# A fused attention and MoE kernel: other rules for interleaving its MoE pieces, a new order of the first blocks, and the last output tile in two halves

## The chip, the cores and the metric

The kernel runs on one core of a Trainium2 chip. The metric is the device time of one execution in microseconds, taken as the median over runs; the kernel before takes 360.17 us (median of 8 runs, 359.39 to 360.54). Engine names are those of the profile: PE multiplies matrices, PEld loads its weights, DVE and ACT are the vector and the scalar engine, POOL is GpSimd, and SP issues DMAs. Each engine runs its instructions in program order and waits on semaphores where the program needs it.

## What is computed

A forgetting attention (8 batches, 8 heads, 576 positions, head size 64) whose output, with the heads put side by side, is the input of a two-layer SiLU block with 2048 hidden channels:

```python
scores = scale * q @ k.T                      # per batch and head
cum    = cumsum(log(clip(f, 1e-4, 1)))
scores = where(causal, scores + cum[:, None] - cum[None, :], -1e9)
attn   = softmax(scores)
x      = (attn @ v).transpose(0, 2, 1, 3).reshape(4608, 512)
h      = x @ moe_w_in                         # 512 -> 2048
out    = (h * sigmoid(h)) @ moe_w_out         # 2048 -> 512
```

## The kernel before, in words

All of it is written as one stream per engine; the order in which the Python code emits instructions is the order in which each engine runs them (`tc.manual_schedule`, line 54). There is no planner that looks at times. What interleaves the two halves of the work is a small accounting function, `fill`, described below.

**Attention.** The decay is folded into the values: each value row and a column of ones beside it is multiplied by a weight computed from `f`, so that one matmul gives numerator and denominator. The 576 positions of a batch are a first block of 128 and a rest of 448.

- *First blocks* (`turn0`, `ban0`, `scores0`, `mask0`, `out0`, `back0`, lines 260 to 365). For each batch b, `turn0(b)` transposes the q and k heads with 32 small matmuls into two PSUM tiles `tp` (one copied out by ACT, one by DVE); `scores0` makes the scores of all 8 heads in one tile `sc` and their exp on ACT; `out0` multiplies by the values into `dn0` and divides on DVE; `back0` transposes the result and copies it into an `x` tile for the MoE. For batches 0 to 3 the causal mask is added in PSUM beforehand (`ban0`), for 4 to 7 it is a DVE multiplication (`mask0`). Batches 0 to 3 run back to back at the start (lines 622 to 668), with a few dummy matmuls (`keep_warm`) between them. Batches 4 to 7 run in `one_more` (line 694) with MoE pieces in between: `fill(0.9)` after `turn0`, `fill(2.0)` after the scores, `fill(1.0)` after `out0`.
- *The rest* (the loop at line 756). It runs over 16 pairs m of head pairs, n = 2m and n + 1. Each `scores(n, c)` for c = 0, 1, 2 fills one of two `sc` buffers (pool `psc`, PSUM banks 0 to 3) with 64-row matmuls (line 433) and gives exps to ACT (lines 437, 449) and mask multiplications to DVE (442, 456). Two such chunks stand together, a "burst" here; a cycle m has three bursts, each followed by a `slot`, then `attend(n)` and `attend(n+1)` (tile `dn`, lines 478 and 487) and a fourth `slot`. `back(m-1)` (tile `tx`, line 508) follows the first slot and writes x. `prepare` issues loads and transposes by DMA (SP), casts (POOL) and value products (POOL) for later n.

**MoE.** The 4608 tokens are cut into 13 groups g of 512, 256, 256, 384 x 4, 256, 384 x 4 and 256 tokens. A piece is one of two kinds:

- M1, `m1_chunk(g, fc)`: 4 matmuls into `hp` (line 532, 128 hidden channels of a group), a tanh on ACT (540) and one DVE instruction (541) that writes `gt`. 16 pieces per group.
- M2, `m2_part(g, tb, part)`: 4 matmuls of 512 columns (558), a quarter of one 128-token output tile `po`. The fourth quarter copies the tile to `osb` on ACT (567) and issues its DMA from SP (570), two DMAs of 64 rows where the tile holds the last 64 tokens of two batches. 4 pieces per 128 tokens.

`hp`, `po`, `dn`, `tx` and `tp` share one pool of four PSUM banks (`pbig`, tag "big", banks 4 to 7). A `po` holds its bank from its first quarter until `osb` has read it.

**The accounting.** `fill(us)` adds to a balance and calls `step()` until the balance is used up; each piece is charged 4 x (columns / 2.4 + 2.5) ns. `step()` emits the next M1 of the running order if its group is ready (`ready`, filled when a group's x has been written), or else the next M2 (of an earlier group than the next M1's; M2 is open from `open2` on, after batch 5). Where both are possible, M1 is taken if its share of the group is not ahead of M2's share (lines 597 to 600). `slot` is `fill` with 1.5 us for m < 2 and 2.5 us later, plus the release of groups. After the loop `step()` runs until nothing is left. The last tile is the second 128 tokens of group 12.

Of the kernel before, what the change touches and what calls it, by code (L numbers as in the profile page):

```python
# [10 lines left out]
FP32 = mybir.dt.float32  # L11
BF16 = mybir.dt.bfloat16
P = 128
# [5 lines left out]
def kernel(  # L19
# [10 lines left out]
    nc = tc.nc  # L30

    B, H, S, D = q.shape
    DM, DFF = moe_w_in.shape
    BH = B * H
    NCC = DM // P
    NFC = DFF // P
# [27 lines left out]
    opool = ctx.enter_context(tc.tile_pool(name="opool", bufs=3))  # L64
# [4 lines left out]
    pbig = ctx.enter_context(tc.tile_pool(name="pbig", bufs=4, space=bass.MemoryType.PSUM))  # L69

    w_in_bf = const.tile([P, NCC, DFF], BF16, name="w_in_bf")
    w_out_bf = const.tile([P, NFC, DM], BF16, name="w_out_bf")
# [17 lines left out]
    GW = [4 * P, 2 * P, 2 * P] + [RB] * NM + [NM * ST] + [RB] * (B - NM) + [(B - NM) * ST]  # L90
    NG = len(GW)
# [13 lines left out]
    def rows_of(g, tb):  # L105

        if g < 3:
            b = tb if g == 0 else 4 + 2 * (g - 1) + tb
            return [(slice(0, P), b, 0)]
        for b in range(B):  # L110
            if REST_OF[b] == g:
                return [(slice(0, P), b, P + tb * P)]
        b0 = (0 if g == 3 + NM else NM) + 2 * tb
        return [(slice(0, ST), b0, SM), (slice(ST, P), b0 + 1, SM)]
# [65 lines left out]
    def load_w_in(i):  # L180
        c0, c1 = i * DFF // WQ, (i + 1) * DFF // WQ
        nc.gpsimd.dma_start(out=w_in_bf[:, :, c0:c1], in_=w_in_v[:, :, c0:c1])
# [27 lines left out]
    for i in range(2):  # L210
        for g in range(2):
            nc.vector.tensor_copy(
                out=sel[:, i, :].rearrange("p (u w r) -> p u w r", u=2, w=2)[:, g, :, :],
                in_=ident_bf[:, :].rearrange("p (r u i w) -> p u i w r", u=2, i=2, w=2)[
                    :, g, i, :, :
                ],
            )

    def keep_warm(n):
        t = pbig.tile([P, SM], FP32, name="wm", tag="big")  # L220
        for _ in range(n):
            nc.tensor.matmul(t[:, :], lhsT=warm[:, 0:P], rhs=warm[:, :], start=True, stop=True)
# [4 lines left out]
        out=f_sb[:, :], in0=f_sb[:, :], scalar1=1e-4, scalar2=1.0, op0=ALU.max, op1=ALU.min  # L227
# [32 lines left out]
    def turn0(b, between=0):  # L260
        src = qk0.pop(b)
        qT0[b] = qktp.tile([P, NP, P], BF16, name="qkT", tag="qkT")
        for i, (dst, evac) in enumerate(
            ((qT0[b], nc.scalar.copy), (kT0[b], nc.vector.tensor_copy))
        ):
            if i == 1 and between:
                keep_warm(between)
            tp = pbig.tile([P, NP, NRUN, RUN], FP32, name="tp", tag="big")
            for c in range(RUN):
                for j in range(2):  # L270
                    nc.tensor.matmul(  # L271
                        tp[j * D : (j + 1) * D, :, :, c].rearrange("p a r -> p (a r)"),
                        lhsT=src[:, i, c * D : (c + 1) * D],
                        rhs=sel[:, j, :],
                        start=True,
                        stop=True,
                    )
            evac(
                out=dst[:, :, :].rearrange("p a t -> p (a t)"),
                in_=tp[:, :, :, :].rearrange("p a r c -> p (a r c)"),  # L280
            )

    def ban0(b):
        sc = psc.tile([P, 2, NP, P], FP32, name="sc", tag="sc")
        for i in range(2):
            nc.tensor.matmul(
                sc[:, i, :, :].rearrange("p a t -> p (a t)"),
                lhsT=ident_bf[:, :],
                rhs=ban[:, :, :].rearrange("p a t -> p (a t)"),
                start=True,  # L290
                stop=False,
            )
        return sc
# [31 lines left out]
    def convert_v0(b):  # L325
        nc.gpsimd.tensor_tensor(
            out=v0[b][:, :, :],
            in0=vf0.pop(b)[:, :, :],
            in1=w_bf[:, 0, b * H : (b + 1) * H, None].to_broadcast([P, H, D + 1]),
            op=ALU.mult,  # L330
        )
# [193 lines left out]
    def m1_chunk(g, fc):  # L525
        w = GW[g]
        if fc == 0:
            gts[g] = gpool.tile([P, NFC, w], BF16, name="gt", tag="gt")
        gt = gts[g]
        hp = pbig.tile([P, w], FP32, name="hp", tag="big")  # L530
        for cc in range(NCC):
            nc.tensor.matmul(  # L532
                hp[:, :],
                lhsT=w_in_bf[:, cc, fc * P : (fc + 1) * P],
                rhs=xg(g)[:, cc, :],
                start=(cc == 0),
                stop=(cc == NCC - 1),
            )
        th = tpool.tile([P, w], BF16, name="th", tag="th")
        nc.scalar.activation(out=th[:, :], in_=hp[:, :], func=ACT.Tanh, scale=0.5)  # L540
        nc.vector.scalar_tensor_tensor(  # L541
            out=gt[:, fc, :],
            in0=th[:, :],
            scalar=1.0,
            in1=hp[:, :],
            op0=ALU.add,
            op1=ALU.mult,
        )
# [2 lines left out]

    def m2_part(g, tb, part):
        gt = gts[g]
        if part == 0:
            pos[g, tb] = pbig.tile([P, DM], FP32, name="po", tag="big")
        po = pos[g, tb]
        for fc in range(4 * part, 4 * part + 4):
            nc.tensor.matmul(  # L558
                po[:, :],
                lhsT=gt[:, fc, tb * P : (tb + 1) * P],  # L560
                rhs=w_out_bf[:, fc, :],
                start=(fc == 0),
                stop=(fc == NFC - 1),
            )
        if part == 3:
            osb = opool.tile([P, DM], FP32, name="osb", tag="osb")
            nc.scalar.activation(out=osb[:, :], in_=po[:, :], func=ACT.Copy, scale=0.5)  # L567
            for r, b, s0 in rows_of(g, tb):
                t0 = b * S + s0
                nc.sync.dma_start(out=out[t0 : t0 + r.stop - r.start, :], in_=osb[r, :])  # L570


    M1 = [(g, fc) for g in range(NG) for fc in range(NFC)]
# [5 lines left out]
        else:  # L579
            M2 += [(g, tb, part) for tb in range(nt) for part in range(4)]  # L580
    M2_OF = [sum(1 for x in M2 if x[0] == g) for g in range(NG)]
    at = {"m1": 0, "m2": 0, "left": 0.0}
    ready: set[int] = set()
    open2 = {"w": False}

    def step():

        a, c = at["m1"], at["m2"]
        can1 = a < len(M1) and M1[a][0] in ready
        g1 = M1[a][0] if a < len(M1) else NG  # L590
        g2 = M2[c][0] if c < len(M2) else NG
        if can1 and M1[a][1] == 0 and g1 > g2 + 1:
            can1 = False
        can2 = open2["w"] and c < len(M2) and g2 < g1
        if not can1 and not can2:
            return None
        if can1 and can2:
            f1 = M1[a][1] / NFC
            f2 = (c - sum(M2_OF[:g2])) / M2_OF[g2]
            can1 = f1 <= f2 or g1 > g2 + 1  # L600
        if can1:
            m1_chunk(*M1[a])
            at["m1"] += 1
            return 4 * (GW[g1] / 2.4 + 2.5)
        m2_part(*M2[c])
        at["m2"] += 1
        return 4 * (DM / 2.4 + 2.5)

    def fill(us_):
        at["left"] += us_ * 1000  # L610
        while at["left"] > 0:
            t = step()
            if t is None:
                at["left"] = 0.0
                return False
            at["left"] -= t
        return True
# [7 lines left out]
        out=ban[:, :, :],  # L625
# [6 lines left out]
    weights()  # L632
    setup_pool.__exit__(None, None, None)
    gpool = ctx.enter_context(tc.tile_pool(name="gpool", bufs=2))
    sc = ban0(0)
    scores0(0, sc)
    keep_warm(1)
    convert_v0(0)
    load_w_in(0)
    turn0(1, between=1)  # L640
    sc = ban0(1)
    scores0(1, sc)
    convert_v0(1)
# [49 lines left out]

    def one_more(b):
        turn0(b)
        fill(0.9)
        scores0(b)
        mask0(b)
        fill(2.0)
        out0(b)  # L700
        fill(1.0)
        back0(b, on_act)

    fill(4.0)
# [41 lines left out]

    pending: list = []

    def slot(us_):
        fill(us_)  # L750
        for x in pending:
            x[0] -= 1
        while pending and pending[0][0] == 0:
            ready.update(pending.pop(0)[1])

    for m in range(NQ):
        n = 2 * m
        piece = 1.5 if m < 2 else 2.5
        scores(n, 0)
        scores(n, 1)  # L760
        prepare(n)
        slot(piece)
        if m > 0:
            back(m - 1)
            if m % 2 == 0:
                b = m // 2 - 1
                pending.append([1, [REST_OF[b]] + ([TAILS_OF[b][0]] if b == NM - 1 else [])])
        scores(n, 2)
        scores(n + 1, 0)
        prepare(n + 1)  # L770
        slot(piece)
        scores(n + 1, 1)
        scores(n + 1, 2)
        slot(piece)
        attend(n)
        attend(n + 1)
        slot(piece)
    back(NQ - 1)
    ready.update([REST_OF[B - 1], TAILS_OF[B - 1][0]])
    for x in pending:  # L780
# [34 lines left out]
```

## Time and profile before

| | us |
|---|---|
| Median of 8 runs (lowest to highest) | 360.17 (359.39 to 360.54) |
| The profiled execution | 359.39 |
| Its span, first to last instruction | 357.6 |
| PE busy in the span | 342.8 (96%) |
| ACT, DVE, POOL busy | 217.0, 189.1, 105.0 |
| First M1 starts at | 20.72 |
| First burst of the loop at | 66.52 |
| Last matmul ends at about | 352.6 |

A profile line of a group reads: line, engine, operation, tile written <- tiles read, shape, xcount | busy us, mean ns of one | idle time of the engine just before, and what ended most of it. In a timeline the first two numbers are the start and the length in us (of all xcount instructions together), and a bracket gives the idle time before and what released the instruction. The 40 digits of a slice row are tenths of busy time, or of granted clock for PEclk. The engines overlap consecutive instructions, so lengths of neighbours may add to more than the time they took together.

### The profile page before, as it was taken

What the parts mean: (1) busy time and instruction counts of PE and PEld (TensorE: products, weight loads), DVE (VectorE), ACT (ScalarE), POOL (GpSimd) and SP (SyncE); (2) the same over time, 40 slices, a digit from 0 to 9 for tenths busy, and PEclk for the clock granted to TensorE, in tenths of its full rate; (3) what the DMA queues carried; (4) which work ended last, traced back from release to release, by engine and by line L of the source; (5) the groups of instructions that cost most, each with busy time, mean ns of one, the idle gap of its engine ahead of it and who ended that gap; (6) DMA issues with size and microseconds to landing.
All of it is one profiled execution on the core that took longest, in us unless ns stands there. A gap on an engine that the chain in (4) does not pass through costs nothing.

```text
span 357.6 us, 8999 instructions
## 1 busy us (share of the span) xinstructions
PE 342.8 (96%) x3632; PEld 202.7 (57%) x3632; DVE 189.1 (53%) x409; ACT 217.0 (61%) x398; POOL 105.0 (29%) x183
## 2 busy tenths in 40 slices
PE   7999898899899999999999999999999999999994
PEld 3644465476566556565655675656656655555651
DVE  4467635366466476555656555456755554344320
ACT  5657454667856767668557677595785644454431
POOL 6992145317254136144116207115400000000000
PEclk9999999999999999999999999999999999999999
DMA  9999989599995698698598878289730101001012
GB/s 159 215 201 202 199 192 205 123 183 168 183 214 119 142 204 185 131 221 135 100 178 154 149 172 176 69 170 191 144 76 7 52 11 59 29 32 59 31 59 60
DMA packets 138809, 47.92 MB, mean 134 GB/s; under 512 B 127952, under 2 KB 134096, under 8 KB 138768
## 3 DMA queue, kind: packets, MB, share of 16 engines
q1 hardware_dynamic: 132240, 41.06, 58.2%
q0 software_dynamic: 6528, 6.29, 10.6%
q8 instruction: 28, 0.46, 0.6%
q14 instruction: 13, 0.11, 0.1%
HBM read 36.85 MB, written 9.44 MB: 129 GB/s over the span
## 4 chain that ended last, share of the span: by engine, by line
PE 81%; ACT 5%; DVE 4%; DMA 4%; issue 2%; SPq 1%; POOL 1%; ACTq 0%; POOLq 0%
PE po L558 32%; PE hp L532 30%; PE sc L433 6%; PE dn L478 4%; PE dn L487 2%; PE tp L271 2%; PE tx L508 2%; DVE gt L541 2%; ACT u L437 2%; DMA qkT<-qkb 2%; DMA qkb<-in_k_dram 1%; DVE xq L350 1%; ACT th L540 1%; DMA vf<-in_v_dram 1%; ACT u L312 1%
## 5 line engine op out<-in xcount | busy, mean ns | idle before, releaser
L532 PE MATMUL hp<-x,w_in_bf 128*128 128x384 bf16 (+2 forms) x832 | 149.9, 314 | 2.1 <-DVE gt L541 1.4
L540 ACT ACTIVATE th<-hp 128x384 bf16<-128x384 f32 (+2 forms) x208 | 96.0, 478 | 88.9 <-PE hp L532 86.5
L541 DVE SCALAR_TENSOR_TENSOR gt<-th,hp 128x384 bf16<-128x384 bf16 (+2 forms) x208 | 106.1, 522 | 79.9 <-ACT th L540 76.8
L558 PE MATMUL po<-w_out_bf,gt 128*128 128x512 bf16 x576 | 145.6, 379 | 0.0
L532 PEld LDWEIGHTS <-w_in_bf 128*128 128x128 bf16 x832 | 77.3, 98 | 58.0 <-issue 3.9
L437 ACT ACTIVATE u<-sc 128x1024 bf16<-128x1024 f32 (+1 forms) x96 | 74.9, 820 | 15.0 <-PE sc L433 14.8
L558 PEld LDWEIGHTS <-gt 128*128 128x128 bf16 x576 | 54.4, 98 | 49.0 <-issue 1.1
L387 POOL TENSOR_TENSOR vp<-vf,w_bf 128x520 bf16<-128x520 f32 (+1 forms) x32 | 35.4, 1107 | 53.4 <-DMA vf<-in_v_dram 38.1
L442 DVE TENSOR_TENSOR u<-u,tri 128x768 bf16<-128x768 bf16 x32 | 20.9, 652 | 23.2 <-ACT u L437 23.2
L567 ACT ACTIVATE osb<-po 128x512 f32<-128x512 f32 x36 | 21.9, 608 | 17.4 <-PE po L558 17.4
L373 POOL CAST qkb<-qf 128x384 bf16<-128x384 f32 x32 | 17.6, 549 | 49.6 <-DMA qf<-in_q_dram 49.0
L433 PE MATMUL sc<-qkT 64*128 64x128 bf16 (+1 forms) x640 | 26.7, 207 | 0.9 <-ACT u L437 0.7
L456 DVE TENSOR_TENSOR ut<-ut,trit 128x128 bf16<-128x128 bf16 x32 | 9.0, 281 | 33.4 <-ACT ut L449 33.3
L433 PEld LDWEIGHTS <-qkT 64*128 64x128 bf16 x640 | 18.3, 94 | 10.1 <-issue 6.9
L449 ACT ACTIVATE ut<-sc 128x640 bf16<-128x640 f32 x32 | 23.1, 722 | 0.0
L478 PEld LDWEIGHTS <-u 128*128 128x128 bf16 x576 | 20.7, 97 | 3.8 <-issue 1.4
L478 PE MATMUL dn<-vp,u 128*128 128x65 bf16 x384 | 21.8, 193 | 0.0
L373 POOL CAST qkb<-kf 128x384 bf16<-128x384 f32 x32 | 17.7, 553 | 11.7 <-DMA kf<-in_k_dram 11.4
L478 PE MATMUL dn<-v,u 128*128 128x65 bf16 x192 | 19.8, 193 | 0.9 <-DVE gt L541 0.9
L496 DVE TENSOR_TENSOR xr<-dn,rec 128x448 bf16<-128x448 f32 x32 | 20.0, 625 | 1.1
L433 PE MATMUL sc<-qkT,kT 64*128 64x64 bf16 (+1 forms) x128 | 16.0, 258 | 0.0
L377 POOL CAST qkb<-qktf 128x128 bf16<-128x128 f32 x32 | 9.4, 294 | 18.2 <-DMA qktf<-in_k_dram 18.2
(64 smaller groups left out, 193.5 us busy)
## 6 DMA issues: line engine op xcount, KB each, us to landing
vf<-in_v_dram SPq DMA_DIRECT2D x32, 256.0 KB, 5.0
out_dram<-osb SPq DMA_DIRECT2D x32, 256.0 KB, 2.1
qf<-in_q_dram SPq DMA_DIRECT2D x64, 96.0 KB, 2.7
kf<-in_k_dram SPq DMA_DIRECT2D x64, 96.0 KB, 2.7
w_in_bf<-in_moe_w_in_dram POOLq DMA_DIRECT2D x4, 512.0 KB, 10.4
w_out_bf<-in_moe_w_out_dram POOLq DMA_DIRECT2D x4, 512.0 KB, 13.9
qkb<-in_q_dram POOLq DMA_DIRECT2D x8, 128.0 KB, 7.3
qkb<-in_k_dram POOLq DMA_DIRECT2D x8, 128.0 KB, 7.7
```

Source lines behind the costliest of these rows:

```text
L373: nc.gpsimd.tensor_copy(out=t2[:, c0 : c0 + NR, :].rearrange("p c x -> p (c x)"), in_=t[:, :, :, :].rearrange("p c h d -> p (c h d)"),)
L387: nc.gpsimd.tensor_tensor(out=vbf[b][r, c, :, :], in0=vst[b][c][r, :, :], in1=w_bf[r, c + 1, b * H : (b + 1) * H, None].to_broadcast([n, H ...
L433: nc.tensor.matmul(sc[:, i, o : o + q1 - q0], lhsT=kt, rhs=t[r, q0:q1], start=True, stop=True)
L437: nc.scalar.activation(out=u[:, :, c * SM : c * SM + w], in_=sc[:, :, 0:w], func=ACT.Exp, scale=scale)
L442: nc.vector.tensor_tensor(out=x, in0=x, in1=tri[:, None, None, :].to_broadcast([P, 2, NR, P]), op=ALU.mult,)
L449: nc.scalar.activation(out=ut[:, :, 0:3:2, :].rearrange("p k i t -> p i k t"), in_=sc[:, :, T0 : T0 + (NM + 1) * ST].rearrange("p i (k t) ...
L478: nc.tensor.matmul(dn[:, i * NR + c - 1, :], lhsT=u[:, i, o : o + P], rhs=vals(kb, i), start=(kb == 0), stop=(kb == c),)
L532: nc.tensor.matmul(hp[:, :], lhsT=w_in_bf[:, cc, fc * P : (fc + 1) * P], rhs=xg(g)[:, cc, :], start=(cc == 0), stop=(cc == NCC - 1),)
L540: nc.scalar.activation(out=th[:, :], in_=hp[:, :], func=ACT.Tanh, scale=0.5)
L541: nc.vector.scalar_tensor_tensor(out=gt[:, fc, :], in0=th[:, :], scalar=1.0, in1=hp[:, :], op0=ALU.add, op1=ALU.mult,)
L558: nc.tensor.matmul(po[:, :], lhsT=gt[:, fc, tb * P : (tb + 1) * P], rhs=w_out_bf[:, fc, :], start=(fc == 0), stop=(fc == NFC - 1),)
L567: nc.scalar.activation(out=osb[:, :], in_=po[:, :], func=ACT.Copy, scale=0.5)
```

## The change

Four places are edited.

1. `step()`: where both kinds are possible and the two shares differ by less than 0.3, the kind that was not emitted last is taken; else the kind that is behind. `fill` and `slot` get an argument `first`, which sets the kind that the slot starts with: M2 in the three slots behind the bursts, M1 in the slot behind `attend`.
2. The first blocks: `turn0(1)` (with `convert_v0(0)` and `load_w_in(0)` ahead of it) is emitted before `ban0(0)` and `scores0(0)`, and two `keep_warm` matmuls go.
3. `one_more`: its three fills grow from 0.9, 2.0 and 1.0 to 1.1, 2.8 and 1.6 us.
4. The last output tile is computed as two halves of 256 columns, one after the other, each with its own bank, eviction and pair of DMAs; the second DMA of each pair is issued by ACT instead of SP.

```diff
     def m2_part(g, tb, part):
         gt = gts[g]
-        if part == 0:
-            pos[g, tb] = pbig.tile([P, DM], FP32, name="po", tag="big")
+        last = g == NG - 1 and tb == GW[g] // P - 1
+        if last:
+            if part % 2 == 0:
+                pos[g, tb] = pbig.tile([P, DM // 2], FP32, name="po", tag="big")
+            m0 = part // 2 * DM // 2
+            m1 = m0 + DM // 2
+            fcs = range(part % 2 * NFC // 2, (part % 2 + 1) * NFC // 2)
+            done = part % 2 == 1
+        else:
+            if part == 0:
+                pos[g, tb] = pbig.tile([P, DM], FP32, name="po", tag="big")
+            m0, m1 = 0, DM
+            fcs = range(4 * part, 4 * part + 4)
+            done = part == 3
         po = pos[g, tb]
-        for fc in range(4 * part, 4 * part + 4):
+        for fc in fcs:
             nc.tensor.matmul(
                 po[:, :],
                 lhsT=gt[:, fc, tb * P : (tb + 1) * P],
-                rhs=w_out_bf[:, fc, :],
+                rhs=w_out_bf[:, fc, m0:m1],
...
-        if part == 3:
-            osb = opool.tile([P, DM], FP32, name="osb", tag="osb")
+        if done:
+            osb = opool.tile([P, m1 - m0], FP32, name="osb", tag="osb")
             nc.scalar.activation(out=osb[:, :], in_=po[:, :], func=ACT.Copy, scale=0.5)
-            for r, b, s0 in rows_of(g, tb):
+            for n, (r, b, s0) in enumerate(rows_of(g, tb)):
                 t0 = b * S + s0
-                nc.sync.dma_start(out=out[t0 : t0 + r.stop - r.start, :], in_=osb[r, :])
+                q_ = nc.scalar if last and n == 1 else nc.sync
+                q_.dma_start(out=out[t0 : t0 + r.stop - r.start, m0:m1], in_=osb[r, :])
...
-            can1 = f1 <= f2 or g1 > g2 + 1
+            can1 = at["last"] == 2 if abs(f1 - f2) < 0.3 else f1 < f2
+        at["last"] = 1 if can1 else 2
...
-    def fill(us_):
+    def fill(us_, first=0):
+        if first:
+            at["last"] = 3 - first
         at["left"] += us_ * 1000
...
+    convert_v0(0)
+    load_w_in(0)
+    turn0(1)
     sc = ban0(0)
     scores0(0, sc)
-    keep_warm(1)
-    convert_v0(0)
-    load_w_in(0)
-    turn0(1, between=1)
     sc = ban0(1)
     scores0(1, sc)
...
     def one_more(b):
         turn0(b)
-        fill(0.9)
+        fill(1.1)
         scores0(b)
         mask0(b)
-        fill(2.0)
+        fill(2.8)
         out0(b)
-        fill(1.0)
+        fill(1.6)
         back0(b, on_act)
...
-        slot(piece)
+        slot(piece, 2)
...
-        slot(piece)
+        slot(piece, 2)
...
-        slot(piece)
+        slot(piece, 2)
         attend(n)
         attend(n + 1)
-        slot(piece)
+        slot(piece, 1)
```

## The prediction

> **What bounds the kernel now.** First the page: which engine is full, and in which slices.
>
> ```profile
> PE 342.8 (96%) x3632; PEld 202.7 (57%) x3632; DVE 189.1 (53%) x409; ACT 217.0 (61%) x398; POOL 105.0 (29%) x183
> PE   7999898899899999999999999999999999999994
> PEclk9999999999999999999999999999999999999999
> L532 PE MATMUL hp<-x,w_in_bf 128*128 128x384 bf16 (+2 forms) x832 | 149.9, 314 | 2.1 <-DVE gt L541 1.4
> L558 PE MATMUL po<-w_out_bf,gt 128*128 128x512 bf16 x576 | 145.6, 379 | 0.0
> L437 ACT ACTIVATE u<-sc 128x1024 bf16<-128x1024 f32 (+1 forms) x96 | 74.9, 820 | 15.0 <-PE sc L433 14.8
> ```
>
> PE is the bound, at full clock; only its waits and the two ends can be saved. A matmul's row (379 ns) is longer than the distance to the next start (216 ns for 512 columns, 162.5 for 384, 109 for 256), so the idle column hides part of each wait. I took the waits as start-to-start distances of PE's rows less these steps. A piece then costs 0.65 us (M1, 384 columns; 0.437 with 256) or 0.864 us (M2). The passages from and to the 64-row scores cost 0.1 us each, in both kernels alike. The waits left over, by stage: start-up to the first M1 at 20.72 us; blocks 4 to 7 (20.7 to 66.5) 4.2 us; the loop (66.5 to 288) 5.8 us; after it none (windows 288:345.7, PE 57.70 of 57.70).
>
> A loop wait, in the timeline of 120.9 to 129.1 us, engine by engine:
>
> ```profile
> 123.98 0.28 PE L433 MATMUL sc<-qkT 64*128 64x64 bf16 x8
> 124.20 2.12 PE L532 MATMUL hp<-x,w_in_bf 128*128 128x384 bf16 x12
> 127.02 0.81 PE L532 MATMUL hp<-x,w_in_bf 128*128 128x384 bf16 x4 [0.70 <-DVE gt L541]
> 124.10 1.30 ACT L437 ACTIVATE u<-sc 128x1024 bf16<-128x1024 f32 x2 [0.59 <-PE sc L433]
> 125.29 0.71 ACT L449 ACTIVATE ut<-sc 128x640 bf16<-128x640 f32 x1
> 125.87 1.28 ACT L540 ACTIVATE th<-hp 128x384 bf16<-128x384 f32 x3
> 126.41 1.48 DVE L541 SCALAR_TENSOR_TENSOR gt<-th,hp 128x384 bf16<-128x384 bf16 x3 [0.16 <-ACT th L540]
> ```
>
> Three M1 stand behind a score burst. Their tanh queues behind the burst's exps, so the first hp bank is free 127.02 - 124.20 = **2.82 us** after the burst, and each further one 0.465 later (three gt in 1.48 with 0.55 for one). An open po holds one of the four banks, so the fourth M1 comes after 3 x 0.65 = 1.95 and waits 0.87. With four banks free it is 2.60 against 2.82: 0.22 (the case at 156 us shows 0.38). With an M2 among the M1 (at 166.84) nothing waits.
>
> **Queued instructions cost less than their rows.** ACT's queue steps on by 0.90 per 1024-wide exp (row 1.031), 0.26 and 0.58 for the two short ones, 0.37 per tanh (row 0.502), 0.48 per osb (0.608): starts above, 125.29 - 124.10 = 1.19 = 0.90 + 0.28. I walk with the steps. The Trainium skill ("ScalarE: Activation LUTs", What ACT_TABLE_LOAD costs) says that back-to-back ACTIVATEs overlap by about 93 ns; these rows show about 0.12. By the page a queue of three exps and three tanh would be some 0.16 us longer, an estimate from its figure.
>
> **The change, part by part**
>
> *Order of the pieces in the loop.* The emission rules are plain arithmetic, so both orders can be written out. The words of the change hold only in part. M2 leads behind 19 of 48 bursts (before: 20). As M2 is taken one for one, though a group has 16 M1 and 12 M2, and as three slots of blocks 4 to 7 take more, M2 runs ahead until the next group is not ready: 14 slots behind bursts hold M1 alone (before 5) and 8 M2 alone (before 3). I walked PE, ACT and DVE through each slot with the steps above and the banks 4 to 7 of the built program. Waits before -> after:
> - m = 0, 1 and m = 2's first half: 0.43 + 0.60 + 0.31 + 0.20 + 0.14 + 0.43 = 2.1 -> 0.3 + 0.92. Osb no longer delays the exps; but six 256-wide M1 around m = 1's third burst make waits of 0.14, 0.19 and 0.59 (second dn).
> - m = 2, 3: 0.87 -> 0.18 + 0.22 (four free banks; the b2 po's are closed).
> - m = 4, 6, 8, third burst: 0.87 + 0.38 + 0.87 -> three times 0.87 (an open po each time).
> - m = 9: 0 -> 0.45: four M1 (2.61) with ACT 0.24 late from an osb and a tanh.
> - m = 11 to 15: 0.43 + 0.16 + 0.06 -> 0.96 (five 256-wide M1: the fifth at 1.75 needs a bank free at 2.71) + 2 x 0.22 (four M1 before back's tx).
> - Sum: 5.8 -> 6.1, **+0.3 us**. Bounds -1.0 (the m = 4, 6, 8 waits at the 0.38 seen) to +2 (ACT 0.5 later in the four M1-only cycles).
>
> SP's queue: the moved M2 take their output DMAs along, and the loads stand behind them. The cover is the lead: a q/k transpose issued at 69.83 had landed at 72.95 and was first needed at 77.25. If it goes, PE waits for qkT as at 87.56 (0.14 us).
>
> *Blocks 4 to 7* (fills 0.9/2.0/1.0 -> 1.1/2.8/1.6). Before: 0.10 + 0.23 + 0.19 (b4), 0.33 + 0.96 (b5), 0.83 + 0.37 + 0.35 (b6), 0.17 + 0.64 (b7) = 4.17. After: b4 0.10 + 0.40, since out0's reciprocal still stands behind the last gt (last hp end to tx: 29.27 to 31.70 = 2.43). b5: group 0's 16 M1 are used up and M2 is not yet open, so the last fill is empty: 2.43 less out0's 0.27 = 2.16. b6: 0 + 0, but block 7's first turn tile now gets the bank of tx and waits for its copy: 1.07 - 0.33 = 0.74. b7: 0, but the first M1 of group 2 now follows back0(7) at once and waits 0.82 for the x copy (56.48 to 57.5 for tx to copied). Sum 4.22: **0.0**. Bounds -1.0 (the two new waits not there) to +0.8.
>
> *Start-up.* turn0(1) goes before block 0's scores; two warm matmuls leave, which opens no gap longer than those under which the clock is granted in full now (1.00 in the window 0:20.72). From the landings of the q and k heads (block 1: 8.61 and 9.14 us; 2: 10.82 and 11.23; 3: 12.11 and 13.12): turn0(1) 8.65 to 9.79, scores0(0) to 10.6, scores0(1) to 11.45 (before 12.29), turn0(2) to 12.47, scores0(2) to 13.65 behind two exps and a copy on ACT (before 14.49), turn0(3) to 14.67, last exp at 16.16 (before 16.97). The rest of the chain follows:
>
> ```profile
> 16.97 1.02 ACT L312 ACTIVATE u<-sc 128x1024 bf16<-128x1024 f32 x1 [0.86 <-PE sc L305]
> 19.65 0.40 PE L362 MATMUL tx<-ident_bf,xq 128*128 128x128 bf16 x4
> 20.72 0.38 PE L532 MATMUL hp<-x,w_in_bf 128*128 128x512 bf16 x1 [0.67 <-ACT x L364]
> ```
>
> First M1 at 19.9 instead of 20.72: **-0.8 us**. POOL's order (convert_v0(0), then w_in's first quarter) is unchanged, and that quarter landed at 18.87: bounds -1.85 and 0.
>
> *Last tile in halves.* 32 matmuls at 0.109 for 16 at 0.216: +0.03. The second half's eviction is 256 wide (row 0.383 against 0.597): -0.21. The tail now:
>
> ```profile
> 352.63 0.60 ACT L567 ACTIVATE osb<-po 128x512 f32<-128x512 f32 x1 [2.85 <-PE po L558]
> 353.25 1.31 SPq L570 DMA_DIRECT2D out_dram<-osb  x2
> ```
>
> SP issued its two DMAs at 353.25 and 354.09, and they landed at 355.71 and 356.37. With the second on ACT's queue both leave at once: about 2.46 after the osb instead of 3.12. The first half's osb and DMAs lie beside 1.74 us of matmuls. Together **-0.8 us**. No row here shows a DMA issued by ACT; nearest are SP's, 0.47 to 0.84 per issue: bounds -1.0 and, if ACT's is slower than SP's second, +0.3. SP's two halves landed 0.66 apart after issues 0.84 apart, so their distance looks like issue time. The Trainium skill speaks against this edit ("DMA: Bandwidth & Descriptors", Rules for kernel authors): transfers to disjoint partition halves serialize on the same DMA engines, and several issuing engines only save issue time. By that rule alone the four smaller DMAs would save no more than the issue step.
>
> **Sum.** +0.3 + 0.0 - 0.8 + 0.03 - 0.8 = **-1.3 us**. The profiled execution took 359.39 (span 357.6 and 1.8 around it), the fastest of eight and 0.8 under their median. Against the median: 360.17 - 1.3 = **358.9 us**.
>
> **Rivals**
> 1. *Slower: ACT falls behind in the M1-only cycles* (m = 3, 5, 7, 9, and m = 1). Behind the third burst the second dn takes the bank of an M1 issued just after the burst: it comes at 1.95 + 0.85 = 2.80 and needs 2.82 + d, where d is how late ACT starts that burst's exps. From d = 0.5 on the gain is gone. With whole rows (1.031, 0.502, 0.553) instead of steps my walk gives d near 0.85 and loop waits of 13.3: 360.17 - 1.6 + 7.5 = **366.0**. For it: those cycles ask ACT for 6 us of exps and 16 tanh in some 14 us. Against it: the steps in the rows above.
> 2. *It does what its words say:* M2 covers each burst's exps and the loop's waits go: 360.17 - 1.6 - 5.8 = **352.8**. For it: bursts led by M2 show no wait. Against it: the order.
> 3. *Nothing comes of the ends:* block 1 starts as late as its DMAs and ACT's queue issues as slowly as SP's second: 360.17 + 0.3 = **360.5**.
>
> **How the numbers follow.** Forecast 0.58 (own range 357.2 to 360.3, from the bounds), rival 1 0.17, rival 2 0.08, rival 3 0.17. The range 356.8 to 361.8 holds the forecast, rival 3 and mild forms of the other two, some 0.8. A change under 0.2% (0.7 us) can hardly be told from none. Faster: 0.8 x 0.58 + 0.08 + a little of rival 3 = 0.56; same: 0.27; slower: 0.17.
>
> **What would show it.** Start-up: first M1 near 19.9. Blocks 4 to 7: a PE gap near 2.1 us at block 5's tx, under 0.2 at out0. Loop: waits of 0.87 at m = 4, 6, 8 and near 1 at m = 11, none over 0.5 in m = 5 and 7. Tail: about 4.5 us from the last matmul's start to the end of the span, where it was 5.4 (352.2 to 357.6). Wrong if dn (L478) waits in m = 5, 7, 9 for a gt over 0.8 us each, if qkT arrives late, or if the ACT-issued DMA lands last by over 0.5 us.

## The result and the profile after

The changed kernel takes **361.38 us** (median of 21 runs, 360.35 to 363.47) against 359.75 for the kernel before (59 runs, 358.69 to 361.06): ratio 1.0051, 95% interval 1.0040 to 1.0061. It is 1.6 us slower; 1.3 us faster was forecast. The profiled execution took 362.94, with a span of 361.2.

The page of the changed kernel, the lines that answer to those shown of before:

```profile
PE 344.5 (95%) x3646; PEld 205.7 (57%) x3646; DVE 185.4 (51%) x409; ACT 217.0 (60%) x399; POOL 102.5 (28%) x183
PE   8999799999899999999999999999999999999995
PEclk9999899999999999999999999999999999999999
L532 PE MATMUL hp<-x,w_in_bf 128*128 128x384 bf16 (+2 forms) x832 | 147.5, 315 | 4.4 <-DVE gt L541 2.9
L570 PE MATMUL po<-w_out_bf,gt 128*128 128x512 bf16 (+1 forms) x592 | 144.0, 376 | 0.0
L437 ACT ACTIVATE u<-sc 128x1024 bf16<-128x1024 f32 (+1 forms) x96 | 74.9, 820 | 22.2 <-PE sc L433 21.8
```

Three things are new: the fifth slice of PE has a hole (a 7), the granted clock falls to 8 in that slice, and L532 waits 2.9 us for gt where it waited 1.4. The waits of PE, longest groups (us in all, times, longest):

```profile
PE hp L532 <- DVE gt L541: 2.9, 4, 0.8
PE tx L362 <- DVE xq L350: 2.3, 2, 2.0
PE sc L433 <- DMA qkT<-qkb: 1.4, 1, 1.4
```

The first line is what was forecast: 0.86 at m = 4, 6 and 8 each and 1.00 at m = 11. The second is block 5's empty fill, forecast too. The third was not: a burst of the loop waits for a q/k transpose.

By stage, in the profiled executions ("beyond pieces" is the stage's length less its pieces at 0.864, 0.650 and 0.436 us each; the pieces are counted from the program, because some of the profiles lack up to 1.4% of the matmul records):

| us | before | changed | no_p3 | fills_67 |
|---|---|---|---|---|
| first M1 at | 20.72 | 20.74 | 20.32 | 19.65 |
| blocks 4 to 7 beyond pieces | 12.47 | 14.25 | 11.90 | 10.70 |
| loop beyond pieces | 69.49 | 72.38 | 66.85 | 67.0 |
| last matmul's start to the span's end | 5.36 | 4.10 | 4.09 | 4.10 |

(no_p3 and fills_67 are experiments below.) Start and tail lost nothing. The blocks lost 1.8 and the loop 2.9.

**Blocks 4 to 7.** PE's timeline at block 5:

```profile
38.68 0.42 PE L340 MATMUL dn<-v,u 128*128 128x65 bf16 x8
41.10 0.56 PE L362 MATMUL tx<-ident_bf,xq 128*128 128x128 bf16 x4 [2.00 <-DVE xq L350]
41.45 1.91 PE L570 MATMUL po<-w_out_bf,gt 128*128 128x512 bf16 x4
43.16 1.06 PE L532 MATMUL hp<-x,w_in_bf 128*128 128x256 bf16 x4
45.17 0.60 PE L532 MATMUL hp<-x,w_in_bf 128*128 128x256 bf16 x4
```

Behind the gap four matmuls of 512 columns take 1.71 us to the next line's start, where they take 0.864 elsewhere, and four of 256 columns 0.85 instead of 0.436. The busy times by window, with the granted clock after the engines' columns, say why:

```profile
37.77:41.18 3.41, 1.41 (x15) 0.77 (x14) 3.06 (x6) 1.28 (x3) 1.10 (x1) 1.00 1.20 192
41.18:44.60 3.42, 3.42 (x14) 1.79 (x15) 0.00 (x0) 0.93 (x2) 0.00 (x0) 0.50 1.23 210
```

For 3.41 us PE had half its clock: matmuls that need 1.7 us took 3.4. The loss read from the starts is 1.55 us.

**The loop.** The burst at 98.26 us (m = 2) stands still in its middle:

```profile
98.35 0.28 PE L433 MATMUL sc<-qkT 64*128 64x64 bf16 x8
100.07 0.40 PE L433 MATMUL sc<-qkT 64*128 64x128 bf16 x8 [1.44 <-DMA qkT<-qkb]
```

From start to start this wait is 1.60. The transpose it waits for was issued at 95.65 and landed at 100.03. Its lateness begins on SP, nearly thirty us earlier. SP's timeline, before and then changed:

```profile
53.25 2.71 SPq L401 DMA_TRANSPOSE qkT<-qkb  x2
56.01 1.26 SPq L171 DMA_DIRECT2D vf<-in_v_dram  x2
57.32 1.15 SPq L150 DMA_DIRECT2D qf<-in_q_dram  x2
```

```profile
54.64 2.72 SPq L401 DMA_TRANSPOSE qkT<-qkb  x2
67.28 1.64 SPq L583 DMA_DIRECT2D out_dram<-osb  x2
68.97 1.19 SPq L171 DMA_DIRECT2D vf<-in_v_dram  x2
70.21 1.15 SPq L150 DMA_DIRECT2D qf<-in_q_dram  x2
```

The larger fills emit the second pair of group 0's output tiles ahead of the loads that follow block 7 in the code. Their DMAs wait on SP for the osb until 67.28, and the loads behind them leave 13.0 us later than before, 11.6 us after the two transposes ahead of them were issued. POOL, which needs the values, waits 18.8 us, and all casts and transposes after it are late:

```profile
72.76 2.18 POOL L387 TENSOR_TENSOR vp<-vf,w_bf 128x520 bf16<-128x520 f32 x2 [18.77 <-DMA vf<-in_v_dram]
```

Less the 1.60, the loop is still 1.3 longer than before.

**How often.** Of the 21 timed executions of the changed kernel, 8 had a granted clock of 0.993 to 0.995 and took 362.06 to 363.47 (median 362.56); 13 had 0.998 to 1.00 and took 360.35 to 361.84 (median 360.98). So the half clock costs about 1.6 us in four of ten executions, about 0.4 in the median, and the kernel is slower without it too.

One execution of the experiment both_mended below, in which the matmuls took two to two and a half times their steps from end to end (443 ns for 512 columns, 390 for 384; 700.69 us), is left out of its numbers, and so is that kernel's profile, which fell on it.

### The profile page after: what moved, and what is told of

Its sections match the earlier page's. It is cut to its first block, busy times and chain, and to the rows that moved or that the text cites. A ratio compares the mean times of both kernels' runs of the same rounds, so it can differ in the third digit from the quotient of the medians.

```text
span 361.2 us, 9032 instructions
## 1 busy us (share of the span) xinstructions
PE 344.5 (95%) x3646; PEld 205.7 (57%) x3646; DVE 185.4 (51%) x409; ACT 217.0 (60%) x399; POOL 102.5 (28%) x183
## 4 chain that ended last, share of the span: by engine, by line
PE 80%; ACT 5%; DMA 4%; DVE 4%; issue 3%; SPq 2%; POOL 1%; POOLq 0%; ACTq 0%
PE po L570 33%; PE hp L532 29%; PE sc L433 6%; PE dn L478 4%; PE dn L487 2%; PE tp L271 2%; DVE gt L541 2%; DMA qkb<-in_q_dram 2%; ACT th L540 2%; PE tx L508 2%; ACT u L437 1%; SPq L150 1%; DMA qkT<-qkb 1%; DMA vf<-in_v_dram 1%; DVE xq L350 1%
## 5 line engine op out<-in xcount | busy, mean ns | idle before, releaser
L532 PE MATMUL hp<-x,w_in_bf 128*128 128x384 bf16 (+2 forms) x832 | 147.5, 315 | 4.4 <-DVE gt L541 2.9
L570 PE MATMUL po<-w_out_bf,gt 128*128 128x512 bf16 (+1 forms) x592 | 144.0, 376 | 0.0
L541 DVE SCALAR_TENSOR_TENSOR gt<-th,hp 128x384 bf16<-128x384 bf16 (+2 forms) x208 | 104.6, 521 | 74.8 <-ACT th L540 72.1
L540 ACT ACTIVATE th<-hp 128x384 bf16<-128x384 f32 (+2 forms) x208 | 94.0, 482 | 77.7 <-PE hp L532 75.9
L532 PEld LDWEIGHTS <-w_in_bf 128*128 128x128 bf16 x832 | 77.5, 98 | 59.2 <-issue 7.7
L570 PEld LDWEIGHTS <-gt 128*128 128x128 bf16 x592 | 56.3, 98 | 50.5 <-issue 2.7
L387 POOL TENSOR_TENSOR vp<-vf,w_bf 128x520 bf16<-128x520 f32 (+1 forms) x32 | 34.5, 1078 | 70.5 <-DMA vf<-in_v_dram 62.9
L579 ACT ACTIVATE osb<-po 128x512 f32<-128x512 f32 (+1 forms) x37 | 21.8, 590 | 23.5 <-PE po L570 23.3
L442 DVE TENSOR_TENSOR u<-u,tri 128x768 bf16<-128x768 bf16 x32 | 19.7, 617 | 30.2 <-ACT u L437 30.2
L373 POOL CAST qkb<-qf 128x384 bf16<-128x384 f32 x32 | 16.6, 518 | 42.3 <-DMA qf<-in_q_dram 41.9
L478 PEld LDWEIGHTS <-u 128*128 128x128 bf16 x576 | 20.9, 97 | 3.7 <-issue 1.0
L373 POOL CAST qkb<-kf 128x384 bf16<-128x384 f32 x32 | 16.5, 517 | 12.0 <-DMA kf<-in_k_dram 12.0
```

The costliest lines, as they stand in the source:

```text
L373: nc.gpsimd.tensor_copy(out=t2[:, c0 : c0 + NR, :].rearrange("p c x -> p (c x)"), in_=t[:, :, :, :].rearrange("p c h d -> p (c h d)"),)
L387: nc.gpsimd.tensor_tensor(out=vbf[b][r, c, :, :], in0=vst[b][c][r, :, :], in1=w_bf[r, c + 1, b * H : (b + 1) * H, None].to_broadcast([n, H ...
L478: nc.tensor.matmul(dn[:, i * NR + c - 1, :], lhsT=u[:, i, o : o + P], rhs=vals(kb, i), start=(kb == 0), stop=(kb == c),)
L532: nc.tensor.matmul(hp[:, :], lhsT=w_in_bf[:, cc, fc * P : (fc + 1) * P], rhs=xg(g)[:, cc, :], start=(cc == 0), stop=(cc == NCC - 1),)
L541: nc.vector.scalar_tensor_tensor(out=gt[:, fc, :], in0=th[:, :], scalar=1.0, in1=hp[:, :], op0=ALU.add, op1=ALU.mult,)
L570: nc.tensor.matmul(po[:, :], lhsT=gt[:, fc, tb * P : (tb + 1) * P], rhs=w_out_bf[:, fc, m0:m1], start=(fc == 0), stop=(fc == NFC - 1),)
```

## The experiments

Times are medians; before is 359.75 (first four), 359.56 (next four) and 359.98 (last four) in the shared runs, so a difference across these groups is sure to about 0.4 us only.

| kernel | us | ratio to before (95%) |
|---|---|---|
| p1_rule: part 1 alone | 356.33 | 0.9909 (0.9894 to 0.9925) |
| p2_start: part 2 alone | 358.72 | 0.9971 (0.9959 to 0.9983) |
| p3_fills: part 3 alone | 365.38 | 1.0160 (1.0136 to 1.0184) |
| p4_tail: part 4 alone | 358.56 | 0.9963 (0.9950 to 0.9975) |
| no_p3: the change without part 3 | 354.68 | 0.9859 (0.9846 to 0.9872) |
| fill_6: the change, one fill 6.0 instead of 11.0 | 354.50 | 0.9869 (0.9849 to 0.9889) |
| loads_early: the change, loads ahead on SP | 360.36 | 1.0023 (1.0006 to 1.0041) |
| hold_clock: the change, dummies in the empty fill | 361.42 | 1.0059 (1.0040 to 1.0077) |
| both_mended: the two repairs together | 359.62 | 0.9990 (0.9976 to 1.0005) |
| lead_16: no_p3 with one fill 16.0 instead of 11.0 | 361.44 | 1.0040 (1.0025 to 1.0054) |
| no_first: no_p3 without `first` | 354.49 | 0.9851 (0.9837 to 0.9864) |
| fills_67: larger fills where M2 is open only | **353.14** | 0.9815 (0.9800 to 0.9830) |

### Each part alone

**p1_rule** adds to the kernel before the new test in `step()` and the argument `first`, as in the diff above, and nothing else.

> The kernel before with the loop's rule alone (part 1 of the change: alternate, M2 first behind each burst), fills, start and last tile as before. Theory A (the loss comes from part 3): output DMAs of group 0's second pair of tiles stay behind the loads on SP, so no qkT is over 0.3 us late, no fill is empty and the clock stays at 1.00; only the loop's own waits grow, from 5.8 to about 6.5: 360.0 to 360.9 us against 359.75 before. Rival B (the order of the loop is the loss): 361.0 to 361.8, with M1-only slots waiting over 0.8 us each in m = 5, 7 and 9.

Measured 356.33: no theory had that. All of them expected a small loss and the rule alone gains 3.4 us. In its profile the loop's waits add up to 3.1 us, where the kernel before has 5.8, and blocks 4 to 7 are 0.6 shorter.

**p2_start** moves `convert_v0(0)`, `load_w_in(0)` and `turn0(1)` ahead of `ban0(0)` and drops the two `keep_warm`.

> The kernel before with the start-up's new order alone (part 2). Theory A: block 1's q landed at 9.51 us in the changed kernel's profile, 0.90 later than in the kernel before, because of the transfers that share its way, so turn0(1) cannot end before 10.5 and the first M1 stays at 20.7: within 0.3 us of before (359.5 to 360.0). Rival C: that late landing was an accident of one execution; then the first M1 comes at 19.9 to 20.3 and the time falls by 0.4 to 0.8 us (358.9 to 359.3).

Measured 358.72, -1.0 us, a little more than rival C's -0.4 to -0.8: rival C is right, the late first M1 in the profile of the changed kernel was a matter of that execution. The chain that ended last, at the start, of the changed kernel and of fill_6, which has the same start-up:

```profile
3.01 6.50 DMA qkb<-in_q_dram
9.55 1.08 PE tp L271 x32
```

```profile
3.00 5.20 DMA qkb<-in_q_dram
8.25 0.64 PE tp L271 x16
```

The same DMA, block 1's q, took 6.50 us in the one execution and 5.20 in the other; the first M1 came at 20.74 and 19.64. In the nine profiles with the new order the first M1 came at 19.62 to 21.12 (mean 20.2), in the four with the old order at 20.72 to 21.10 (mean 20.9). The new order is worth 0.7 to 1.0 on average and puts this DMA's landing on the path.

**p3_fills** is the kernel before with one edit:

```diff
-        fill(0.9)
+        fill(1.1)
...
-        fill(2.0)
+        fill(2.8)
...
-        fill(1.0)
+        fill(1.6)
```

> The kernel before with the larger fills alone (part 3). Theory A: this part carries the loss in two ways. Block 5's last fill is empty, PE has a gap of about 2.1 us, and in some 4 of 10 executions a stretch of 3.4 us at half clock follows (1.7 us each time); and the second pair of output DMAs comes ahead of the loads for n = 2 and 3 on SP, so that a qkT is 0.5 to 2 us late in m = 1 or 2. 361.0 to 362.5 us, granted clock 0.995 in some runs and 1.00 in others, 1.7 us apart. Rival B (the loop's order is the loss): 359.6 to 360.2.

Measured 365.38, +5.6: theory A has the right part, but priced it at half or less. A late transpose is there (0.62 in m = 2), the gap of 2.16 at block 5 too; they don't make 5.6. In its profile (364.24, the fastest of six executions, clock 0.998) blocks 4 to 7 are 1.0 longer than before and the loop, beyond its pieces, 3.5. The loop's waits add up to 9.1 instead of 5.8, and four of them are new: 0.94, 0.93, 0.94 and 0.94 behind runs of M1 at the first two bursts of m = 5 and the first bursts of m = 7 and 9, where the kernel before does not wait. PE's lines at m = 5 (a score burst stands ahead of each run of M1):

```profile
138.21 2.12 PE L532 MATMUL hp<-x,w_in_bf 128*128 128x384 bf16 x12
141.11 0.81 PE L532 MATMUL hp<-x,w_in_bf 128*128 128x384 bf16 x4 [0.78 <-DVE gt L541]
142.77 2.12 PE L532 MATMUL hp<-x,w_in_bf 128*128 128x384 bf16 x12
145.66 0.81 PE L532 MATMUL hp<-x,w_in_bf 128*128 128x384 bf16 x4 [0.76 <-DVE gt L541]
```

**p4_tail** has the new `m2_part` alone.

> The kernel before with the last tile in two halves alone (part 4). Theory A: the end comes 4.1 to 4.3 us after the start of the last matmul instead of 5.4: -1.1 us, 358.5 to 358.8. Rival: the smaller DMAs share the same way and save only SP's issue step of 0.84 less what ACT's issue costs: -0.5, 359.2.

Measured 358.56, -1.2 us, as theory A said. The end of the changed kernel:

```profile
357.37 0.38 ACT L579 ACTIVATE osb<-po 128x256 f32<-128x256 f32 x1 [1.36 <-PE po L570]
357.78 0.51 ACTq L583 DMA_DIRECT2D out_dram<-osb  x1
```

SP issued its half at 357.78 as well; they landed at 359.72 (SP) and 360.00 (ACT). No run has the two halves without the second queue, or the queue without the halves, so how the 1.2 us divide between them is not shown.

The four parts alone add up to -3.4 - 1.0 + 5.6 - 1.2 = 0.0; together they give +1.6. So they are not independent, and a new theory was needed: **the larger fills let M2 run ahead before the loop, and that spoils the loop's order**, under either rule. What stands ahead of the loop is called the lead here. The programs' own orders show it. Before the loop stand 31 M1 and 15 M2 in the kernel before, 30 and 15 in p1_rule, 36 and 18 in p3_fills, 34 and 19 in the changed kernel. Third bursts that have three or more M1 directly behind them: 4 in the kernel before (m = 2, 4, 6 and 8, with waits of 0.87, 0.87, 0.38 and 0.87), 2 in p1_rule (m = 13 and 15: 0.27 and 0.38), 7 in the changed kernel. p3_fills has 4 too; its new runs stand behind first and second bursts, so all three bursts of a cycle have to be counted: 4 in the kernel before, 6 in p1_rule (none of which waits more than 0.38), 11 in p3_fills, 15 in the changed kernel. With M2 ahead, M2 of the old group is used up early, a run of M1 alone must bring the next group, then a run of M2 alone follows.

### Without the lead, and with the lead alone

**no_p3** undoes part 3; **fill_6** leaves it in and takes the lead away with one number.

```diff
-    fill(11.0)
+    fill(6.0)
```

> The changed kernel without part 3 (fills back to 0.9, 2.0 and 1.0 us; the three other parts stay). Theory A (part 3 is the loss, and it also spoils part 1: with the larger fills M2 runs ahead before the loop, so 14 slots behind bursts are M1 alone and 8 M2 alone, against 5 and 3 with the old fills): the three parts add up to -3.4 - 1.0 - 1.2, so 354.1 us (353.6 to 354.8), loop waits about 3. Rival B (the three parts do not add up, for instance because the earlier start is lost again at a transfer): 355.2 or more.

> The changed kernel with one number altered: the fill after block 5 is 6.0 instead of 11.0 us, so that as many pieces stand ahead of the loop as in the kernel before (30 M1 and 15 M2). The larger fills around blocks 4 to 7 stay, with the empty one. Theory A (the harm of part 3 comes through M2's lead, and the loads' place on SP with it): loop waits 3 to 4 us instead of 8.6, no late qkT, the half clock after the empty fill still in some executions: 355.0 to 356.5. Rival D (the larger fills do their harm on the spot, in blocks 4 to 7): above 359.

no_p3 measured 354.68: the three other parts add up to within 0.7 (4.9 under the kernel before of the same runs, where the parts alone gave 5.6). fill_6 measured 354.50, even below its expectation, with the larger fills and the empty one in place; rival D falls. Five of its six executions had a clock of 1.00 and took 354.34 to 354.94, the sixth 0.995 and 356.76. Its loop has one late transpose (1.43 at m = 2).

The same third burst (m = 4) of the changed kernel and of no_p3, PE's lines:

```profile
132.03 2.12 PE L532 MATMUL hp<-x,w_in_bf 128*128 128x384 bf16 x12
134.85 0.81 PE L532 MATMUL hp<-x,w_in_bf 128*128 128x384 bf16 x4 [0.70 <-DVE gt L541]
```

```profile
122.04 1.47 PE L532 MATMUL hp<-x,w_in_bf 128*128 128x384 bf16 x8
123.56 0.81 PE L570 MATMUL po<-w_out_bf,gt 128*128 128x512 bf16 x3
```

Three M1 and a fourth that waits for a bank, against two M1 and then an M2, which needs no new bank while the burst's exps pass.

**lead_16** goes the other way: no_p3, the loads ahead of block 7 so that SP is no cause, and the lead put back.

```diff
-    fill(11.0)
+    fill(16.0)
...
+    load_v(0, 2)
+    load_v(0, 3)
+    load_qk(2)
+    load_qk(3)
+    load_tails(1)
     one_more(7)
-    load_v(0, 2)
-    load_v(0, 3)
-    load_qk(2)
-    load_qk(3)
...
-    load_tails(1)
```

> The kernel no_p3 (old fills, no empty one) with one number raised: the fill after block 5 is 16.0 instead of 11.0 us, so that 33 M1 and 19 M2 stand ahead of the loop, nearly as in the changed kernel; the loads stand ahead of block 7, so that SP's queue is no cause. 14 slots behind bursts are then M1 alone and 8 M2 alone, again as in the change. Theory A (the lead of M2 spoils the order, wherever it comes from): loop waits of 6.5 or more instead of 3, 357.0 to 359.0 us. Rival D (the larger fills do the harm on the spot, in blocks 4 to 7): 354.5 to 355.5.

Measured 361.44: the lead alone costs 6.8 us (6.3 when each is taken against the kernel before of its own runs), with the old fills around the blocks, no empty one and no late loads. That is more than theory A's 357 to 359, and rival D is out. The waits of PE in lead_16, then in no_p3:

```profile
PE dn L478 <- DVE gt L541: 3.0, 6, 0.8
PE hp L532 <- DVE gt L541: 1.7, 2, 1.0
```

```profile
PE dn L478 <- DVE gt L541: 1.0, 2, 0.8
```

Start to start, lead_16's loop waits add up to 8.3 and no_p3's to 3.1. Beyond its pieces the loop of lead_16 is 5.3 longer (72.1 against 66.85), and the waits make 5.2 of that: 4.4 are waits for a gt, behind M1, and 0.8 are bursts of m = 0 and 1 that wait longer for an exp. Blocks 4 to 7 are 0.85 longer, and the first M1 was 0.8 later in that execution. Every kernel with a lead has both more M1 (33 to 36 against 30 or 31) and more M2 (18 or 19 against 15) ahead of the loop; which of the two does the harm no run separates.

### The two other losses

**loads_early** moves the same loads (and `load_tails(1)`) ahead of `one_more(7)` in the changed kernel, as in the diff of lead_16. **hold_clock** covers the gap:

```diff
-        fill(1.6)
+        if not fill(1.6):
+            keep_warm(10)
```

> The changed kernel with the loads of n = 2 and 3, of the last two value blocks and of the second tails ahead of block 7, so that on SP they stand before the second pair of output DMAs; the order on PE, ACT and DVE is that of the changed kernel. Theory A1 (SP's queue carries most of the loop's loss): the qkT wait of 1.6 us in m = 2 goes, 359.6 to 360.3. Theory A2 (the M1-only slots carry most, the late qkT is a matter of single executions): 360.6 to 361.2.

> The changed kernel with ten dummy matmuls of 512 columns (2.2 us) in the place of the empty fill of block 5. Theory A (the gap of 2.15 us takes the clock to half for 3.4 us in some 4 of 10 executions): no execution under 0.996 granted, the upper group of times (362 to 363.5) is gone, median 360.7 to 361.1. Rival E (the low clock has nothing to do with that gap): times from 360.4 to 363.5 as before, with clocks of 0.993 to 0.995 in some. If the dummies delay the transposes behind them by more than 0.1 us, that much is added.

> The changed kernel with both repairs at once: the loads ahead of block 7 (as in loads_early) and ten dummy matmuls in the empty fill (as in hold_clock). The order of the pieces stays that of the change. Theory A: loads_early had two groups, 359.4 to 359.8 at a clock of 0.998 or more and 360.9 to 361.9 at 0.994 or 0.995; with the gap covered only the lower one is left: median 359.4 to 359.9, no execution under 0.997. What is then left of the loss, about 5 us above no_p3, is the order. Rival F (the dummies themselves cost time, as hold_clock's median of 361.4 may say): 360.3 or more without any low clock.

loads_early measured 360.36 in two groups: 359.37 to 359.78 at a clock of 0.998 or more (six executions, median 359.70) and 360.93 to 361.92 at 0.994 or 0.995 (six, median 361.49). Against the changed kernel's 360.98 and 362.56 each group is 1.1 to 1.3 lower (the kernel before was 0.2 lower in these runs too): that is about what the loads behind the output DMAs cost. On SP the loads now leave at 56.53 and the output DMAs stand behind them:

```profile
56.53 1.26 SPq L171 DMA_DIRECT2D vf<-in_v_dram  x2
66.80 1.66 SPq L583 DMA_DIRECT2D out_dram<-osb  x2
```

hold_clock measured 361.42 (360.96 to 363.01): none of its six executions was under 0.998, as theory A says, but the median is 0.3 above theory A's range and 0.4 above the changed kernel's group at full clock, which six executions cannot settle; the slowest, 363.01, had a clock of 1.00, so a time like those of the upper group came without the low clock. Its PE lines at block 5, where the dummies end just before the transposes, show that they delay nothing:

```profile
37.82 2.32 PE L222 MATMUL wm<-warm 128*128 128x512 bf16 x10
39.98 0.40 PE L362 MATMUL tx<-ident_bf,xq 128*128 128x128 bf16 x4
```

In its profile two bursts of m = 2 wait for late transposes, 0.89 and 1.12, together 2.0 instead of 1.6: as long as SP is late, part of what PE wins ahead of the loop is given back there.

With both repairs the time is 359.62, ten of eleven executions at 0.998 or more (358.55 to 359.82), as theory A expected; rival F falls. One execution had 0.994 and 361.43 although the gap is filled; that one stays unexplained. What then remains above fill_6, which has the same larger fills but not the lead, is 359.6 - 354.5 = 5.1 us (4.7 when each is taken against the kernel before of its own runs); it goes with the lead.

### What of the rule gains, and a faster kernel

**no_first** is no_p3 with `slot(piece)` four times. **fills_67** is the changed kernel with the old fills around blocks 4 and 5, the larger ones around 6 and 7, and `fill(8.0)` after block 5:

```diff
     def one_more(b):
+        f0, f1, f2 = (0.9, 2.0, 1.0) if b < 6 else (1.1, 2.8, 1.6)
         turn0(b)
-        fill(1.1)
+        fill(f0)
...
-        fill(2.8)
+        fill(f1)
...
-        fill(1.6)
+        fill(f2)
...
-    fill(11.0)
+    fill(8.0)
```

> The kernel no_p3 without the argument first of slot and fill: the kinds still alternate, but M2 is first behind 13 bursts instead of 21. Theory A (what the rule gains is the alternation, and M2 first behind the burst adds to it where a slot has both): 354.8 to 355.6. Rival G (M2 first behind the burst is what gains): 356.5 or more, most of part 1's 3.4 us lost.

> The changed kernel with the larger fills only around blocks 6 and 7, where M2 is open, and the fill after block 5 cut to 8.0 us, so that 30 M1 and 15 M2 stand ahead of the loop as in the kernel before; no fill is empty. Theory A: fill_6's 354.4 less its gap of 2.15 us at block 5, plus the waits of blocks 4 and 5 with the old fills (1.8 in the kernel before, of which fill_6 has 0.5): 353.3 to 354.2, no low clock. Rival (what is won ahead of the loop is lost again at a qkT that its loads pace, as fill_6's wait of 1.4 us at 84.7 us shows): 354.4 to 355.0.

no_first measured 354.49, no_p3 354.68: M2 first behind 13 bursts or behind 21 makes no difference that these runs show. It is the alternation while the shares are within 0.3 that gains; "M2 first" was the part of the change's words to leave out. fills_67 measured 353.14, 6.8 under the kernel before (359.98) and the fastest here. Its five executions had 0.999 or 1.00; in its profile blocks 6 and 7 wait for 0.7 us instead of the 2.4 of the kernel before, blocks 4 and 5 keep their 1.7 (0.96 of it at block 5's tx), and the lead is the old one (30 M1, 15 M2).

## Why the prediction was wrong, point by point

The forecast summed +0.3 (loop), 0.0 (blocks), -0.8 (start), -0.8 (tail). The two profiled executions are 3.6 apart instead of -1.3 (loop +2.9, blocks +1.8, start 0.0, tail -1.3); the medians 1.6.

- **Tail, -0.8: right in sign, too small.** Measured 4.10 instead of 5.36 from the last matmul's start to the end, and -1.2 alone. From the first issue to the last landing it took 2.22 where it took 3.12 before and 2.46 was reckoned, and the shorter last matmul gives 0.10. No run shows the bound of +0.3, an ACT queue that is slower. The rule of the Trainium skill that spoke against the edit ("DMA: Bandwidth & Descriptors", Rules for kernel authors) allows just the issue time as the gain. SP's issue step before was 0.84, so up to that much of the 1.26 can be issue time; the shorter eviction gives 0.21, and no run separates the parts further.
- **Start, -0.8: right on average** (-1.0 alone), and its condition was named, the landing of block 1's q and k. In the profiled execution that DMA landed at 9.51 instead of 8.61 and the gain was 0. That the clock is full in 0:20.72 was read too kindly: in the profile before, the first dummy matmuls step by 0.427 instead of 0.216 until 4.6 us. Nothing in the sum rests on it.
- **Blocks 4 to 7, 0.0: the walk was right, the clock was missing.** Idle time at block 4 was 0.09 + 0.43 (said: 0.10 + 0.40), at block 5's tx 2.16 (2.16), at block 7's turn 0.79 (0.74), at back0(7) 0.84 (0.82). But the 2.16 was priced as idle time alone, a term for the clock was not in the sum; the half clock after it costs another 1.6 in four of ten executions.
- **Loop, +0.3: this is the step that failed most; the loop lost 2.9.** The walk itself held at the places named (0.86 at m = 4, 6, 8; 1.00 at m = 11; 0.45 at m = 9) and was 0.8 short in all (6.9 instead of 6.1, most of it in m = 0 and 1). What failed was "SP's queue ... The cover is the lead: a q/k transpose issued at 69.83 had landed at 72.95 and was first needed at 77.25. If it goes, PE waits for qkT as at 87.56 (0.14 us)". The two output DMAs were not followed to the place where they stand in SP's order, ahead of the loads after block 7. There they held the loads for 11.6 us, and the price is 1.60 in the profile and 1.1 to 1.3 in the medians. One of the prediction's own signs of being wrong, a late qkT, is what came. Most of the rest of the miss is the walk: loads_early has neither late loads nor, in half of its executions, a low clock, and these (median 359.70) still don't beat the kernel before of the same runs (359.56); its loop is 1.4 longer beyond its pieces than before, where +0.3 was said.
- **The split into parts was not made.** Rule and fills were walked only together, so the sum could not show that one gives 3.4 and the other takes 5.6. The fact that decides was in the text ("M2 runs ahead until the next group is not ready"), as a reason why the words of the change hold only in part; it was put down to the rule and the larger fills at once and priced for neither. With the same rule and fill_6's smaller lead the kernel takes 354.50.
- **The rivals.** Rival 2 (the waits go, 352.8) comes nearest without part 3, where they do not go but shrink: loop waits of 3.1 instead of 5.8, 354.7. Rival 1 named the right place, M1-only cycles, and the right wait, dn for a gt (0.57 at m = 1, 0.45 at m = 9), but ACT is not late by 0.5 there. Rival 3 did not occur: both ends gain when tried alone (-1.0 and -1.2).

Left open: whether the M1 or the M2 of the lead does the harm, the one low clock in both_mended, and the one slow execution of hold_clock at full clock.

## What to carry to other kernels

Walk each part of a change alone before walking them together; where one part feeds pieces to the place that another part orders, the stock that it leaves (here 34 M1 and 19 M2 instead of 31 and 15) is a quantity of its own, to be written down at the border between the stages. For every DMA that moves with a moved piece, write its queue's new order down to the first load behind it, and ask until when the DMA itself must wait. An idle gap of PE can cost more than its length, where it falls inside one window of the granted clock (2.16 us did here, 1.17 did not): fill it with dummies, or better, keep pieces for it.

## What the runs showed of the hardware

The clock of PE is granted in windows of 3.41 us: the whole stretches of half clock last that long, and the stretches of full clock are multiples of it. The grid lies differently in each execution (borders at 37.77 and 41.18 in the changed kernel; 37.03 and 40.44 in p3_fills, reckoned back from the fall at its end). Four profiles have the gap at block 5, 2.19 us from start to start and 2.16 less the step. In two it lies inside one window (38.91 to 41.10 in 37.77 to 41.18; 38.42 to 40.61 in 38.16 to 41.57) and the next window has half the clock; in the other two a border falls into it (39.28 to 41.47 with 40.44; 37.81 to 40.00 with 39.40) and the clock stays full. A gap of 1.17 inside a window of the kernel before (37.33 to 38.50 in 35.36 to 38.77) did not lower the clock.

The ends of the kernels, where PE falls idle, give more windows. PE was busy for 0.53 us in the window 354.96 to 358.37 of hold_clock and for 0.95 in 348.06 to 351.47 of no_first, and the clock fell at the end of each; it stayed full behind 1.81 us (no_p3, 347.20 to 350.62) and 1.88 us (fills_67, 345.40 to 348.81). At block 5, 1.41 us were too few (both low cases) and 1.71 us enough (p3_fills, 40.44 to 43.85). In all 13 profiles no window behind the start-up breaks this: half clock follows where PE was busy for 1.41 us or less, full clock where it was busy for 1.71 or more. If the grid lies at random, the gap falls whole into one window with a chance of (3.41 - 2.16) / 3.41 = 37%; counted were 8 of 21, 6 of 12 and 1 of 6 low executions in the changed kernel, loads_early and fill_6, 15 of 39. (p3_fills is not counted: its clocks, 0.993 to 0.998, make no two groups.) So one kernel can have two times 1.6 us apart.

The Trainium skill ("TensorE: Matmul & The Clock Gate", Part 1: The HAM clock gate) has the free-running window of about 3.4 us, which agrees; it puts the fall to half clock after an idle window, and its list of advice ("Why this matters for your kernels") warns of gaps over about 3 us. Here a gap of 2.16 was enough, in a window in which PE was busy for 1.41 of 3.41 us.
